# Early tiles' choices inside the retention, a reordered list, and weight loads that wait for the first gather

## The chip, the cores and the metric

One core of one Trainium2 chip runs the whole program. The metric is device time in microseconds (us), the median of several runs. TensorE (PE in the rows) does matrix products, with the loading of its weights as PEld; VectorE (DVE), ScalarE (ACT) and GpSimd (POOL) do elementwise work; SyncE (SP) issues most DMAs. Each engine works through its own instructions in order and waits for the others by semaphores. 16 DMA engines move all data between HBM and the on-chip memory.

## What is computed

Three stages follow each other. The middle one is a mixture of experts with a capacity, assigned greedily over all logits:

```python
scores = (q @ k.T) / sqrt(64) * decay          # retention, 8 heads, causal decay
x = (scores @ v)                               # 2304 tokens x 512
logits = x @ w_gate                            # 8 experts
for idx in argsort(-logits.flatten()):         # strongest pair first
    tok, e = idx // 8, idx % 8
    if assigned[tok] >= 0 or counts[e] >= 288: continue
    assigned[tok] = e; counts[e] += 1
for e in range(8):
    out[mask_e] = maximum(x[mask_e] @ w1[e], 0) @ w2[e]     # 512 -> 1024 -> 512
h = out @ w_in                                 # 512 -> 2048
result = (h * tanh(log1p(exp(h)))) @ w_out     # 2048 -> 512
```

## The kernel before

**Retention.** 18 tiles of 128 tokens run one after the other. For tile t the loop (lines 280 to 289) issues loads, the scores of tile t+1, the outputs of tile t, the running state, and `turn(t - 1)`: that transposes the tile, adds its logits to `L` (a VectorE reduction, line 254) and stores its rows of x to `x_scratch`. The order of PE, DVE and POOL here is the order of the program text.

**Routing.** The greedy assignment is done expert by expert in the order in which they fill up. `choices` (L350 to L355) finds each token's best open expert with five small DVE instructions, `reached` (L361) compares each best logit with 63 thresholds into the table `G`, and TensorE counts with `pF` (L305, L445) how many tokens of each expert lie above each. Six such steps (`route`, DVE table `G` L427, PE `pF`, DVE `sat`, PE `pD`) narrow down the threshold at which the next expert is full. `weights_of` then reads that expert's number (`eid`) and loads its weights, and `tokens` makes the list of its 288 tokens: comparisons, the table `ohb` in two halves (L587), the PE product `pI` (L595), the list `chosen` (L599). Three indirect DMAs on POOL (L607) gather the rows of x (`xg`), PE transposes them (`mmx`), and ACT and DVE split them into a rounded part and a rest (`xh`, `xl`).

**Experts.** Each expert needs eight weight units of 512 KB (`st`, line 543): four of w1, four of w2. ACT rounds a unit (`whi`, L557); POOL or DVE forms the rest (`wlo`, L560). Every product takes three TensorE passes (high by high, low by high, high by low): `mma` is the first layer, `mmb` the second, 96 matmuls each. A unit of w1 serves two of the first layer's eight blocks. Five staging buffers (`STAGES`) hold loaded units. Beside this, `narrow` turns the last stage's weights from 64-bit words into f32 (`std`, `words`, `dw`, `dt`), a piece at a time.

**The planner.** After the retention the order on every engine is made by a list scheduler at build time (`run_tasks`). A task yields (engine, assumed duration in ns, what it waits for, priority); the smallest start time goes first, and a task steps back for one of smaller priority number that would be ready before it ends. Assumed times only set the order. Among them are `LATE` (8,000 ns, added to the arrival of most loads) and `GATHER` (10,000 ns from the gather's issue to its rows). Before expert 0's first product PE runs dummy products (`warm`).

Of the kernel before, what the change touches and what calls it, by code (L numbers as in the profile page):

```python
# [17 lines left out]
P = 128  # L18
# [8 lines left out]
HP = H // 2  # L27
WARM = 11
STRADDLE = (4, 13)

# [15 lines left out]
LATE = 8000  # L46
GATHER = 10000
SCATTER = 3200
FIRST = 163
# [83 lines left out]
class Kernel:  # L133
# [3 lines left out]
    def attention(self):  # L137
# [10 lines left out]
        with ExitStack() as st:  # L148
# [129 lines left out]
            scale(1, nc.gpsimd)  # L278
            scale(2, nc.gpsimd)
            for t in range(NT - 1):  # L280
                load(t + 3)
                scale(t + 3, nc.gpsimd)
                scores(t + 1)
                carried(t, Sb[seen[0] % 2])
                outputs(t)
                state(t)
                turn(t - 1)
                if t == 6:
                    self.routing_consts()
            t = NT - 1  # L290
            carried(t, Sb[seen[0] % 2])
            outputs(t)
            turn(t - 1)
            self.psum = lambda name, shape: ps.tile(shape, F32, name=name, tag="pS" if name == "pF" else "pA", bufs=1 if name == "pF" else 2)
            G = self.rw.tile([P, NT, 64], BF16, name="G")
            self.chosen = self.rw.tile([GB, E, 3], I32, name="chosen", bufs=1)
            pF = self.psum("pF", [64, E])
            early, late = slice(0, t - 1), slice(t - 1, NT)
            choice = self.choices(early)
            self.reached(choice, G, early)  # L300
            turn(t)
# [41 lines left out]
    def choices(self, ts=slice(0, NT), into=None):  # L343

        pool, v, L = self.rw, self.nc.vector, self.L
        both = [P, ts.stop - ts.start, E]
        if into is None:
            into = [self.at("raw"), pool.tile([P, NT], F32, name="top"), pool.tile([P, NT, E], BF16, name="oh")]
        raw, top, oh = (x[:, ts] for x in into)
        v.tensor_reduce(raw, L[:, ts], AX.X, ALU.max)  # L350
        cand = self.at("cand").rearrange("p (t e) -> p t e", e=E)[:, ts]
        v.tensor_tensor(cand, L[:, ts], raw[:, :, None].to_broadcast(both), op=ALU.is_equal)
        v.tensor_tensor(cand, cand, self.rc[:, None, RC["prio"]].to_broadcast(both), op=ALU.mult)
        v.tensor_reduce(top, cand, AX.X, ALU.max)
        v.tensor_tensor(oh, cand, top[:, :, None].to_broadcast(both), op=ALU.is_equal)  # L355
        return into

# [11 lines left out]
    def route(self):  # L369
# [8 lines left out]
        for i in range(E):  # L378
# [102 lines left out]
            if i:  # L481
                self.widen(i, ohe)
                self.spawn(self.weights_of(junk, at, i))
                choice = yield from self.choose(i, at)
            at = yield DVE, 1600, [marked, at], 0
            pose = rw.tile([P, NT], F32, name="pose")
            v.scalar_tensor_tensor(pose, scan[:, 1], pP[:, 1:2], eq, op0=ALU.add, op1=ALU.mult)
            v.scalar_tensor_tensor(pos, scan[:, 0], pP[:, 0:1], gt, op0=ALU.add, op1=ALU.mult)
            fin = self.at("fin")
            v.scalar_tensor_tensor(fin, pose, CAP + 0.5, eq, op0=ALU.is_lt, op1=ALU.mult)  # L490
            if i == 0:
                self.spawn(self.weights_of(junk, at, i))
            v.tensor_tensor(self.dead, self.dead, gt, op=ALU.add)
            v.tensor_tensor(self.dead, self.dead, fin, op=ALU.add)
            v.tensor_tensor(pose, pose, fin, op=ALU.mult)
            v.tensor_tensor(pos, pos, pose, op=ALU.add)
            self.spawn(self.tokens(i, pos, at))
            if i == 0:
# [11 lines left out]
    def choose(self, i, at):  # L510
        if i == E - 2:
            return None
        yield DVE, 1750, [at], 0
        return self.choices()

    def weights_of(self, junk, at, i):
# [11 lines left out]
        for u in range(8):  # L528
            if u < 4:
                src = a["w1"][bass.ds(e, 1), :, u * 256:(u + 1) * 256]  # L530
            else:
                src = a["w2"][bass.ds(e, 1), (u - 4) * 256:(u - 3) * 256, :]
            yield from self.unit(n0 + u, src.rearrange("o (k p) c -> p (o k) c", p=P),
                                 DVE if n0 == 0 and u < 2 else None, units, 3,
                                 *([lambda: self.fetched] if n0 == 0 and u == FIRST_UNITS else []))

    def unit(self, n, src, eng, into, prio, *after):
# [4 lines left out]
        st = self.stage.tile([P, 1024], F32, name="st")  # L542
        self.nc.sync.dma_start(st.rearrange("p (k c) -> p k c", k=src.shape[1]), src)
        self.loaded[n] = at
        self.spawn(self.split_unit(n, st, self.arrival(524288, at, LATE if 1 < n < E * 8 else DMA_WAIT), eng, into, prio))

    def split_unit(self, n, st, at, eng, into, prio):
# [10 lines left out]
        self.rounded[n] = hi  # L558
        lo = yield ({POOL: 2480, DVE: 1240} if eng is None else eng), 1240, [hi], prio
        (self.nc.vector if lo.engine == DVE else self.nc.gpsimd).tensor_tensor(dst[1], st, dst[0].bitcast(F32), op=ALU.subtract)  # L560
# [3 lines left out]
    def tokens(self, i, pos, at):  # L564
# [24 lines left out]
        for ts, made in zip(halves, ready):  # L589
            at = yield PE, 740, [made, side, *([] if pI is not None else [self.bank])], pr  # L590
            if pI is None:
# [14 lines left out]
        for j in range(3):  # L606
            nc.gpsimd.indirect_dma_start(out=xg[:, j], out_offset=None, in_=a["x"],  # L607
                                         in_offset=bass.IndirectOffsetOnAxis(ap=idx[:, j:j + 1], axis=0))
        at = Event(at.t + GATHER)
        if i > 1:  # L610
# [499 lines left out]
```

## Time and profile before

| | us |
|---|---|
| median of 3 runs (lowest, highest) | 813.99 (812.19, 814.79) |
| profiled execution | 809.8 |
| its span, first to last instruction | 808.0 |
| PE busy | 766.4 (95% of the span) |
| DVE busy | 668.5 (83%) |
| POOL busy | 464.4 (57%) |
| ACT busy | 413.2 (51%) |
| mean granted TensorE clock | 0.982 of full |

The span is one profiled execution; its own time is a little above its span. Busy time of an engine counts its instructions, not its waits. The retention ends at about 84 us, expert 0's products start at 126.03 us, and the last stage begins to dominate after about 390 us.

### The profile page before, as it was taken

Reading aid. Unit: us, or ns where it says so; the run is one execution under the profiler, and the core shown is the slowest. Engines: PE = TensorE matmul, PEld = TensorE weight load, DVE = VectorE, ACT = ScalarE, POOL = GpSimd, SP = SyncE. Lnnn points to the kernel's source line nnn. Section 1 sums busy time; section 2 is a strip of 40 time slices with the busy share of each in tenths; the row PEclk is TensorE's granted clock in tenths of the full one; section 3 lists DMA queues with packets and bytes.
Section 4 is the critical chain, followed back from the end, with each engine's and each line's share of the span. In section 5 each row is a group of like instructions: output and inputs, shape, how many; then the busy total and the mean of one; then the engine's idle time right before and its main releaser. Section 6 shows DMA issues by size and latency. Waiting matters only on the chain.

```text
span 808.0 us, 16171 instructions
## 1 busy us (share of the span) xinstructions
PE 766.4 (95%) x6184; PEld 688.3 (85%) x6184; DVE 668.5 (83%) x1089; ACT 413.2 (51%) x781; POOL 464.4 (57%) x402
## 2 busy tenths in 40 slices
PE   7999479999999999799899899999999999999996
PEld 5898338898999989799898788898899988999985
DVE  2444687897988888696698999989998998998993
ACT  1233115556555565575664455555556556555552
POOL 3653035779797796340166776657466566655644
PEclk9999789999999999899999999999999999999999
DMA  9993165888888887986700010001001001000001
GB/s 342 408 354 129 41 208 184 265 264 283 252 290 251 299 265 229 331 270 231 247 1 21 20 40 21 12 21 47 2 20 40 19 21 40 20 1 13 27 1 39
DMA packets 61117, 112.52 MB, mean 139 GB/s; under 512 B 4848, under 2 KB 33008, under 8 KB 61040
## 3 DMA queue, kind: packets, MB, share of 16 engines
q1 hardware_dynamic: 44816, 74.00, 26.8%
q10 hardware_dynamic: 13248, 28.06, 10.4%
q0 software_dynamic: 2976, 9.44, 3.6%
q8 instruction: 48, 0.79, 0.4%
q14 instruction: 29, 0.24, 0.1%
HBM read 88.93 MB, written 22.54 MB: 138 GB/s over the span
## 4 chain that ended last, share of the span: by engine, by line
PE 59%; DVE 8%; DMA 2%; POOL 2%; issue 2%; ACT 1%; SPq 0%; POOLq 0%; ACTq 0%; DVEq 0%
PE mmc L987 23%; PE po L1048 21%; PE mmb L771 7%; PE mma L771 7%; DVE q L1017 2%; DMA st<-w 1%; PE pF L445 1%; DVE hl L797 1%; DVE ohb L587 1%; DVE wlo L560 1%; DVE G L427 1%; DMA st<-w_out 1%; POOL n L1019 1%; POOL gl L1029 1%; DVE n L1012 1%
## 5 line engine op out<-in xcount | busy, mean ns | idle before, releaser
L1017 DVE RECIPROCAL q<-q 128x384 f32<-128x384 f32 x96 | 244.3, 2545 | 11.3 <-ACT q L1015 9.7
L1019 POOL TENSOR_TENSOR n<-n,q 128x384 f32<-128x384 f32 x96 | 99.3, 1034 | 140.3 <-DVE q L1017 137.7
L1029 POOL TENSOR_TENSOR gl<-n,gh 128x384 fp32r<-128x384 f32 x96 | 105.4, 1098 | 50.5 <-ACT gh L1027 50.1
L987 PE MATMUL mmc<-yl,whi 128*128 128x384 f32 x384 | 130.2, 339 | 4.3 <-POOL yl L947 2.5
L987 PE MATMUL mmc<-yh,whi 128*128 128x384 f32 x384 | 130.0, 339 | 0.6 <-ACT yh L944 0.5
L987 PE MATMUL mmc<-yh,wlo 128*128 128x384 f32 x384 | 129.7, 338 | 0.0
L560 POOL TENSOR_TENSOR wlo<-st,whi 128x1024 fp32r<-128x1024 f32 x49 | 116.9, 2400 | 13.1 <-ACT whi L557 12.4
L1048 PE MATMUL po<-whi,gh 128*128 128x512 f32 x288 | 114.0, 396 | 0.0
L1048 PE MATMUL po<-whi,gl 128*128 128x512 f32 x288 | 113.9, 395 | 0.0
L1048 PE MATMUL po<-wlo,gh 128*128 128x512 f32 x288 | 113.3, 393 | 0.0
L1005 ACT ACTIVATE s<-mmc 128x384 f32<-128x384 f32 x96 | 47.1, 491 | 122.2 <-PE mmc L987 119.2
L1012 DVE SCALAR_TENSOR_TENSOR n<-s 128x384 f32<-128x384 f32 x96 | 103.3, 1076 | 2.1 <-ACT s L1005 1.2
L557 ACT CAST whi<-st 128x1024 fp32r<-128x1024 f32 x80 | 82.0, 1043 | 40.5 <-DMA st<-w 31.6
L771 PE MATMUL mma<-xh,whi 128*128 128x288 f32 x256 | 77.5, 303 | 3.0 <-DVE xl L620 3.0
L987 PEld LDWEIGHTS mmc<-yl,whi 128*128 128x128 f32 x384 | 72.1, 188 | 9.5 <-POOL yl L947 3.4
L771 PE MATMUL mmb<-hl,whi 128*128 128x288 f32 x256 | 77.9, 304 | 0.0
L771 PE MATMUL mmb<-hh,whi 128*128 128x288 f32 x256 | 77.4, 302 | 0.0
L771 PE MATMUL mmb<-hh,wlo 128*128 128x288 f32 x256 | 77.3, 302 | 0.0
L987 PEld LDWEIGHTS mmc<-yh,whi 128*128 128x128 f32 x384 | 72.1, 188 | 5.5 <-ACT yh L944 1.5
L771 PE MATMUL mma<-xh,wlo 128*128 128x288 f32 x256 | 76.7, 300 | 0.0
L771 PE MATMUL mma<-xl,whi 128*128 128x288 f32 x256 | 76.6, 299 | 0.0
L987 PEld LDWEIGHTS mmc<-yh,wlo 128*128 128x128 f32 x384 | 72.2, 188 | 0.0
(146 smaller groups left out, 1541.2 us busy)
## 6 DMA issues: line engine op xcount, KB each, us to landing
st<-w SPq DMA_DIRECT2D x64, 512.0 KB, 5.7
qk<-qk SPq DMA_DIRECT2D x18, 512.0 KB, 7.9
kv<-kv SPq DMA_DIRECT2D x18, 512.0 KB, 8.1
std<-w_out ACTq DMA_DIRECT2D x15, 512.0 KB, 5.1
std<-w_in ACTq DMA_DIRECT2D x14, 512.0 KB, 5.3
x_scratch<-xs SPq DMA_DIRECT2D x18, 256.0 KB, 4.1
y_scratch<-y ACTq DMA_DIRECT2D x32, 144.0 KB, 3.9
yt<-y_scratch SPq DMA_DIRECT2D x22, 192.0 KB, 2.4
```

Of the source, the lines that this page charges most:

```text
L427: v.tensor_tensor(G[:, :, :m], key[:, :, None].to_broadcast([P, NT, m]), T[:, None, :].to_broadcast([P, NT, m]), op=ALU.is_ge)
L445: nc.tensor.matmul(pF[:m, :], G[:, t, :m], oh[:, t, :], start=(t == 0), stop=(t == NT - 1))
L557: self.nc.scalar.copy(dst[0], st)
L560: (self.nc.vector if lo.engine == DVE else self.nc.gpsimd).tensor_tensor(dst[1], st, dst[0].bitcast(F32), op=ALU.subtract)
L771: self.nc.tensor.matmul(bank[1][:, :CAP], al if h == 2 else ah, bl if h == 1 else bh, start=(first and j == h == 0), stop=(last and j == n ...
L987: self.nc.tensor.matmul(bank[1][:, :TILE], (wl if h == 2 else wh)[:, c, cs], x[c][h == 1], start=(c == h == 0), stop=(c == HP - 1 and h == 2))
L1005: nc.scalar.activation(s, p, AF.Sigmoid)
L1012: v.scalar_tensor_tensor(u, s, 2.0, s, op0=ALU.subtract, op1=ALU.mult)
L1017: v.reciprocal(q, q)
L1019: nc.gpsimd.tensor_tensor(u, u, q, op=ALU.mult)
L1029: nc.gpsimd.tensor_tensor(gl, u, gh.bitcast(F32), op=ALU.subtract)
L1048: nc.tensor.matmul(po[j], (gl if h == 2 else gh)[:, js], (wl if h == 1 else wh)[:, f % 2], start=(f == h == 0), stop=(f == DFF // P - 1 an ...
```

## The change

Five edits are made together.

1. The choices and the first threshold table of tiles 0 to 8, 9 to 12 and 13 to 15 are made inside the retention loop, right after `turn` of the last of them, rather than for tiles 0 to 15 in one go after `turn(16)` and ahead of `turn(17)`. The last two tiles are done after `turn(17)` as before.
2. In `route`, the two updates of `dead` come after the positions that the list needs, and in a request of their own; `choose` of expert 0 is split into two requests; the planner assumes 480 ns for `pI` rather than 740.
3. The `wlo` of expert 0's units 0 and 1 goes from DVE to POOL, and is planned after the gather.
4. The load of unit 2 of expert 0 (`FIRST_UNITS` is 2) gets a semaphore wait on the last of the first gather's three DMAs. SP issues in order, so all later loads follow it.
5. The planner assumes 3,000 ns (`GATHERED`) for the first gather's landing rather than 10,000, and plans unit 2 after that.

```diff
+EARLY = (9, 13, 16)
+GATHERED = 3000
...
+            G, choice = self.rw.tile([P, NT, 64], BF16, name="G"), None
             for t in range(NT - 1):
...
+                if t in EARLY:
+                    ts = slice(max([0] + [e for e in EARLY if e < t]), t)
+                    choice = self.choices(ts, choice)
+                    self.reached(choice, G, ts)
...
-            early, late = slice(0, t - 1), slice(t - 1, NT)
-            choice = self.choices(early)
-            self.reached(choice, G, early)
+            late = slice(EARLY[-1], NT)
             turn(t)
             self.choices(late, choice)
...
-            at = yield DVE, 1600, [marked, at], 0
+            at = yield DVE, 1250, [marked, at], 0
...
             v.scalar_tensor_tensor(fin, pose, CAP + 0.5, eq, op0=ALU.is_lt, op1=ALU.mult)
+            v.tensor_tensor(pose, pose, fin, op=ALU.mult)
+            v.tensor_tensor(pos, pos, pose, op=ALU.add)
             if i == 0:
                 self.spawn(self.weights_of(junk, at, i))
+            self.spawn(self.tokens(i, pos, at))
+            at = yield DVE, 350, [at], 0
             v.tensor_tensor(self.dead, self.dead, gt, op=ALU.add)
             v.tensor_tensor(self.dead, self.dead, fin, op=ALU.add)
-            v.tensor_tensor(pose, pose, fin, op=ALU.mult)
-            v.tensor_tensor(pos, pos, pose, op=ALU.add)
-            self.spawn(self.tokens(i, pos, at))
...
-        yield DVE, 1750, [at], 0
-        return self.choices()
+        if i:
+            yield DVE, 1750, [at], 0
+            return self.choices()
+        at = yield DVE, 650, [at], 0
+        parts = self.choice_parts()
+        into = next(parts)
+        yield DVE, 1000, [at], 0
+        next(parts, None)
+        return into
...
-                                 DVE if n0 == 0 and u < 2 else None, units, 3,
-                                 *([lambda: self.fetched] if n0 == 0 and u == FIRST_UNITS else []))
+                                 POOL if n0 == 0 and u < FIRST_UNITS else None, units, 3,
+                                 *([lambda: self.fetched and Event(self.fetched.t + GATHERED)] if n0 == 0 and u == FIRST_UNITS else []))
...
+        if n == FIRST_UNITS:
+            self.tc.add_manual_dep(d.ins, self.gathering.name, mybir.DependencyInfo(mybir.DependencyClass.Sync, mybir.DependencyReason.DATA),
+                                   reason="the first expert's rows go ahead of its later weights")
...
-        lo = yield ({POOL: 2480, DVE: 1240} if eng is None else eng), 1240, [hi], prio
+        lo = yield ({POOL: 2480, DVE: 1240} if eng is None else eng), 2480 if eng == POOL and n < E else 1240, [hi, *([lambda: self.fetched] if n < FIRST_UNITS else [])], prio
...
-            at = yield PE, 740, [made, side, *([] if pI is not None else [self.bank])], pr
+            at = yield PE, 480, [made, side, *([] if pI is not None else [self.bank])], pr
...
-        at = Event(at.t + GATHER)
+        at = Event(at.t + (GATHER if i else GATHERED))
```

`choice_parts` is `choices` as a generator that pauses after the `is_equal` of L352; `choices` runs it to its end.

## Rows read from the trace of the kernel before

**Rows 1.** Stages: from:to length, PE PEld DVE ACT POOL busy, clock, DMA share, GB/s.
```profile
80.00:126.00 46.00, 28.37 (x341) 17.56 (x340) 32.88 (x119) 7.31 (x15) 6.27 (x4) 0.81 0.45 148
126.00:330.00 204.00, 201.41 (x1948) 187.38 (x1946) 174.60 (x550) 117.41 (x205) 161.21 (x93) 1.00 0.79 256
330.00:340.00 10.00, 4.74 (x28) 3.95 (x28) 4.28 (x7) 5.18 (x11) 1.27 (x1) 0.77 1.06 387
340.00:808.00 468.00, 456.95 (x2397) 415.19 (x2396) 422.55 (x343) 261.03 (x486) 258.79 (x255) 1.00 0.16 53
```

**Rows 2.** Timeline at the retention's end: start, duration, engine, line, operation [idle before].
```profile
82.15 2.12 PE L252 MATMUL pX<-both,xT 128*128 128x136 f32 x16
83.47 0.28 DVE L350 TENSOR_REDUCE sc<-L 128x16 f32<-128x128 f32 x1
...
84.98 1.20 DVE L361 TENSOR_TENSOR G<-sc,rc 128x1008 bf16<-128x1008 f32 x1
86.10 0.17 DVE L254 TENSOR_REDUCE L<-pX 128x8 f32<-128x16 f32 x1
```

**Rows 3.** Timeline inside the retention, at tile 15.
```profile
69.41 1.29 DVE L204 TENSOR_TENSOR am<-pA,mask 128x512 f32<-128x512 f32 x2 [0.85 <-PE pA L201]
```

**Rows 4.** Timeline from the first decision to the list of expert 0.
```profile
104.91 0.17 DVE L493 TENSOR_TENSOR dead<-dead,sc 128x18 f32<-128x18 f32 x1
...
109.22 0.57 PE L595 MATMUL pI<-R,ohb 128*96 128x6 bf16 x9 [0.16 <-DVE ohb L587]
...
110.81 0.15 DVE L599 TENSOR_REDUCE chosen<-pI 96x3 int32<-96x6 f32 x1
```

**Rows 5.** Timeline from the first gather to expert 0's first product.
```profile
111.24 1.10 POOL L607 DMA_INDIRECT xg<-x_scratch,chosen  x1 [39.98 <-DMA st<-w]
...
114.71 1.07 POOL L607 DMA_INDIRECT xg<-x_scratch,chosen  x1 [0.30 <-issue]
...
126.03 0.38 PE L771 MATMUL mma<-xh,whi 128*128 128x288 f32 x1
```

**Rows 6.** DMA of 114 to 118 us: queue shares, and issue to landing.
```profile
q0 software_dynamic: 84, 0.28, 23.1%
...
xg<-x_scratch,chosen POOLq DMA_INDIRECT x2, 8.6
```

**Rows 7.** DMA of 310 to 345 us: the last two experts' gathers.
```profile
xg<-x_scratch,chosen POOLq DMA_INDIRECT x6, 3.8
```

**Rows 8.** The gathers (tile xg) over the span: issue durations, and landing.
```profile
L607 POOL DMA_INDIRECT xg<-x_scratch,chosen x24: 917/921/1961, 111.2 to 323.3; - x24
...
DMA to landing us min/median/max: 3.1/5.0/8.8
```

**Rows 9.** The staged weights (tile st), 100 to 150 us: landing.
```profile
DMA to landing us min/median/max: 3.5/6.7/10.2
```

**Rows 10.** The page's groups: cost of rounding a unit and of its rest.
```profile
L560 POOL TENSOR_TENSOR wlo<-st,whi 128x1024 fp32r<-128x1024 f32 x49 | 116.9, 2400 | 13.1 <-ACT whi L557 12.4
...
L557 ACT CAST whi<-st 128x1024 fp32r<-128x1024 f32 x80 | 82.0, 1043 | 40.5 <-DMA st<-w 31.6
```

**Rows 11.** Timeline of ACT in expert 0's first layer: blocks three and four.
```profile
132.43 0.41 ACT L794 ACTIVATE hh<-mma 128x288 fp32r<-128x288 f32 x1 [1.48 <-PE mma L771]
134.18 0.41 ACT L794 ACTIVATE hh<-mma 128x288 fp32r<-128x288 f32 x1 [1.34 <-PE mma L771]
```

**Rows 12.** Timeline of PE where expert 1 begins.
```profile
159.76 0.66 PE L628 MATMUL mmx<-cst,xg 96*128 96x96 f32 x6
...
160.83 0.30 PE L771 MATMUL mma<-xh,whi 128*128 128x288 f32 x1
```

**Rows 13.** The chain that ended last, in the steady part: start, duration, what.
```profile
218.03 0.73 PE pF L445 x18
```

**Rows 14.** Timeline of POOL: the first multiplication of `narrow`.
```profile
148.38 1.29 POOL L754 TENSOR_TENSOR dw<-dw,dt 128x512 f32<-128x512 f32 x1
```

**Rows 15.** Timeline of PE: expert 0's second layer, its 37th matmul.
```profile
147.55 0.30 PE L771 MATMUL mmb<-hh,whi 128*128 128x288 f32 x1
```

More of the change, by code (lines that the diff above doesn't have):

```diff
@@ L294, in attention @@
             self.psum = lambda name, shape: ps.tile(shape, F32, name=name, tag="pS" if name == "pF" else "pA", bufs=1 if name == "pF" else 2)
-            G = self.rw.tile([P, NT, 64], BF16, name="G")
             self.chosen = self.rw.tile([GB, E, 3], I32, name="chosen", bufs=1)
             pF = self.psum("pF", [64, E])
-            early, late = slice(0, t - 1), slice(t - 1, NT)
-            choice = self.choices(early)
-            self.reached(choice, G, early)
+            late = slice(EARLY[-1], NT)
             turn(t)
@@ L343, in choices, with choice_parts @@
     def choices(self, ts=slice(0, NT), into=None):
+        parts = self.choice_parts(ts, into)
+        into = next(parts)
+        next(parts, None)
+        return into
+    def choice_parts(self, ts=slice(0, NT), into=None):
         pool, v, L = self.rw, self.nc.vector, self.L
@@ L352, in choices @@
         v.tensor_tensor(cand, L[:, ts], raw[:, :, None].to_broadcast(both), op=ALU.is_equal)
+        yield into
         v.tensor_tensor(cand, cand, self.rc[:, None, RC["prio"]].to_broadcast(both), op=ALU.mult)
@@ L355, in choices @@
         v.tensor_tensor(oh, cand, top[:, :, None].to_broadcast(both), op=ALU.is_equal)
-        return into
     def reached(self, choice, G, ts):
@@ L512, in choose @@
             return None
-        yield DVE, 1750, [at], 0
-        return self.choices()
+        if i:
[3 more added lines that the diff above has]
+        parts = self.choice_parts()
+        into = next(parts)
+        yield DVE, 1000, [at], 0
+        next(parts, None)
+        return into
     def weights_of(self, junk, at, i):
@@ L542, in unit @@
         st = self.stage.tile([P, 1024], F32, name="st")
-        self.nc.sync.dma_start(st.rearrange("p (k c) -> p k c", k=src.shape[1]), src)
+        d = self.nc.sync.dma_start(st.rearrange("p (k c) -> p k c", k=src.shape[1]), src)
+        if n == FIRST_UNITS:
+            self.tc.add_manual_dep(d.ins, self.gathering.name, mybir.DependencyInfo(mybir.DependencyClass.Sync, mybir.DependencyReason.DATA),
+                                   reason="the first expert's rows go ahead of its later weights")
         self.loaded[n] = at
@@ L606, in tokens @@
         for j in range(3):
-            nc.gpsimd.indirect_dma_start(out=xg[:, j], out_offset=None, in_=a["x"],
+            d = nc.gpsimd.indirect_dma_start(out=xg[:, j], out_offset=None, in_=a["x"],
                                          in_offset=bass.IndirectOffsetOnAxis(ap=idx[:, j:j + 1], axis=0))
-        at = Event(at.t + GATHER)
+        self.gathering = d.ins
+        at = Event(at.t + (GATHER if i else GATHERED))
         if i > 1:
```

## The prediction, made before the result

> **What bounds the kernel now.** I read the table of stages first. In the last stage, from 340 us, PE is busy for 457 of 468 us; while the experts are worked through beside the routing, from 126 to 330 us, it is busy for 201.4 of 204. The change touches neither's work. Between the retention's end and the first product PE is busy for only 28.4 of 46 us, dummy products included, and from 330 to 340 us for 4.7 of 10 [rows 1]. So a start of expert 0's products that comes earlier by some us is worth as much at the end, unless a wait behind it takes it back. The timelines of those 46 us then show one chain: the retention's last choices, the threshold search, the list, the gather, the first product. The reader is to see in them which piece of work stood in front of which [rows 2, 4, 5]. The DMA views say why the rows of the gather were late [rows 6 to 9].
>
> **What it takes off that chain.** (1) PE ends the last `turn` at 82.15 + 2.12 = 84.27, but DVE adds that tile's logits only at 86.10, since the choices and the table of sixteen tiles run from 83.47 to 84.98 + 1.20 = 86.18 in front of it [rows 2]. With those made before, the reduction can start at about 84.35: 1.75 us. The moved work, 2.7 us in one go, comes as three pieces of nine, four and three tiles. I cost it at nothing, because DVE idles 0.85 us ahead of each tile's `am` [rows 3] and the nine-tile piece, by its share of 2.7 some 1.5 us and with its fixed costs perhaps 2, delays one `am` by about 1 us, which is needed a tile later. If that cover is gone the three cost at most 3 x (2 - 0.85), 3.5 us; bounds 0 and 3.5, and I take 0.
>
> (2) The two updates of `dead`, 0.17 us each, stood in front of the positions [rows 4]: 0.3 us. The list's end, `chosen`, started at 110.81 although PE had finished its counts at 109.22 + 0.57 = 109.79 [rows 4]: DVE was in the five instructions of the next choice, one request of 1,750 ns for the planner. Split in two, with 480 ns for the product, the list is ready for the planner before the first half would end, so it goes first: 1.0 us. The other experts' lists also gain 0.3 each, beside a busy PE; I count nothing for them.
>
> (3) The three gathers started 114.71 - 111.24 = 3.47 us apart from first to last, 0.30 of it idle ahead of the third [rows 5]; one takes 0.92 as a rule, though up to 1.96 [rows 8]. DVE's two `wlo` ran beside these three; they leave. At the usual pace the third starts after 2 x (0.92 + 0.30) = 2.4; I take 2.6, a gain of 0.85, bounds 0 and 1.0.
>
> (4) Landing. The first gathers took a median of 8.6 us, in a window whose other traffic was weights [rows 6]. The last two experts' gathers took 3.8 [rows 7]; the quickest of all 3.1, the median 5.0 [rows 8]. With only two weight units ahead of them, I take 3.8: a gain of 4.8, bounds 3.6 and 5.5. The share of the gather's queue in that window is 23.1% [rows 6]. The Trainium skill, page "DMA: Bandwidth & Descriptors", section "Queues, rings and completion order", says that each DMA engine takes turns between the queues that have work, a packet at a time. By that rule a gather with a queue of its own needn't be protected from another queue's weights, and the whole 4.8 would be in doubt; the measured share and the two landing times speak for protection, and the trace does not separate them from other causes.
>
> Together 1.75 + 0.3 + 1.0 + 0.85 + 4.8 = 8.7 us: the first product would start at 117.3 rather than 126.03 [rows 5].
>
> **What it adds.** (a) Unit 2 waits. The gather starts at 111.24 - 3.05 = 108.2, its third DMA at 110.8, and lands at 114.6; only then does SP issue unit 2 and, behind it, units 3 to 7 and the first three loads of `narrow`. Landing takes 3.5 us at best and 6.7 at the median [rows 9], rounding 1.04, the rest on POOL 2.40 [rows 10]: ready at 121.6 to 124.8. The fifth block of the first layer needs it. The fourth block's activation came at 134.18, 8.15 us after the first product [rows 5, 11], so the need is at about 117.3 + 8.15 = 125.4. That alone would be no wait. But the planner still adds `LATE`, 8,000 ns, to the unit's arrival, and so puts its rounding on ACT behind the third block's activation. That one came 6.4 us after the start [rows 11], now 123.7 to 124.1; rounding ends at 125.2, the rest at 127.6: PE waits 2.2 us. Behind the fourth activation it would be 3.9. Bounds 0 and 3.9, I take 2.2.
>
> (b) Before, PE ran five of the six `pF` steps of expert 1's search while it had nothing else to do; with an earlier start some three of them fall beside products, at 0.73 us each [rows 13]: 2.2 us if all of it is new PE time, 0 if they fall into the waits (a) and (c), which are longer together. I take 1.0.
>
> (c) PE now reaches expert 1 earlier, but expert 1's list does not come earlier by as much: its search gains the 1.75, 0.3 and 1.0, and DVE loses two splits, yet it now shares DVE with expert 0's work. Before, the transposes of expert 1 stood inside expert 0's last products, 1.07 us ahead of the first `mma` [rows 12]. If they come behind them, PE waits for their splitting; from landed rows to the first product expert 0 needed 126.03 - (114.71 + 8.6) = 2.7 [rows 5, 6]. Bounds 0 and 2.7, I take 1.5.
>
> (d) POOL gets 2 x 2.40 = 4.8 us of splits [rows 10]. Units 0 and 1 are split from about 112 to 117, before the first product needs the second of them; the cover is the gather's flight.
>
> So 8.7 - 2.2 - 1.0 - 1.5 = 4.0 us less: 805.8 against the profiled execution's 809.8. That execution lay below the median of the runs, 813.99; I take the same difference from the median: 810.0.
>
> **The rivals.** *The lead arrives whole.* Unit 2 is rounded in time and the search keeps up, so (a) and (c) vanish: 8.7 - 1.0 = 7.7, 806.3; with the bounds of the gains, 0.15 + 0.7 more, and part of the 2.6 us in which PE idled from 126 to 330 [rows 1], 803.5. For it: the unit's data are there 0.6 us or more ahead of need. Against it: ACT is in order and the planner's 8,000 ns stand.
>
> *The wait at expert 6 swallows it.* From 330 to 340 us PE idles 5.3 us while the DMA engines are fully busy [rows 1]. If the transfers there keep their place on the clock, PE merely arrives earlier and waits longer; perhaps 1 us stays: 813.0. Against it: the DMA share is 0.79 on average before, so there is room for an earlier transfer.
>
> *The gather is no faster.* If the gather's queue already got its turns beside the weights and the 8.6 had another cause, the 4.8 goes; the waits shrink with the lead, (a), (b) and (c) to about 2 in all: 8.7 - 4.8 - 2 = 1.9 less at best, some 1 to 2, about 813. The 23.1% of a queue that had three transfers waiting [rows 6] makes that unlikely. It is the rule of the Trainium skill's page "DMA: Bandwidth & Descriptors" ("Queues, rings and completion order") taken at its word.
>
> *Slower: POOL becomes the bound of expert 0.* Six units are split on POOL, 6 x 2.40 = 14.4 us [rows 10]. Where the first starts at 127, behind the fourth activation, and three multiplications of `narrow` at 1.29 [rows 14] come between, the last unit is done at 127 + 14.4 + 3.9 = 145.3, and the gather of expert 1 stands behind it on POOL. The second layer needs that unit for its 37th matmul, which came 147.55 - 126.03 = 21.5 us after the first product [rows 5, 15], now 138.8: 6.5 us of waiting. If expert 1's rows come late by the gather's own issue too, (c) is at its bound of 2.7. 8.7 - 6.5 - 2.2 - 2.7 = 2.7 slower: 816.7. It decides once the waits of (a), (b), (c) together pass 8.7. Against it: a split takes 2.40, and PE used a unit of w1 in two blocks, 8.15 / 2 = 4.1 us [rows 11], so a late start is caught up.
>
> **How the numbers follow.** Forecast 0.49, own range 808.0 to 812.0; lead whole 0.16; swallowed 0.14; gather no faster 0.06; slower 0.15. About 0.3%, 2.4 us, is what a measurement of this kernel can tell from no change. Of the forecast's 0.49 some 0.05 lie within it: faster 0.44 + 0.16 = 0.60, same 0.05 + 0.14 + 0.06 = 0.25, slower 0.15. The range reaches from the lead's far end, 803.5, to 816.0, about the middle of the slower case, and leaves out some 0.15.
>
> **What would show it.** The last tile's logits at about 84.4; `chosen` at about 107.8; gathers landing in 3 to 5 us; first `mma` near 117.3; an idle of about 2 us on PE ahead of the fifth block, ended by a `wlo` of POOL; the first `mma` of expert 1 at about 155 (before: 160.83); the idle of 330 to 340 us at its former length, moved forward. It is wrong if the first `mma` comes after 120, if PE waits for units 3 to 7 as well, or if expert 6 begins when it began before.

## The result, and the profile after

The changed kernel took 825.15 us (median of 4 runs, 824.65 to 829.36) against 813.45 before in the same session: a ratio of 1.0146, 95% interval 1.0119 to 1.0172. The profiled execution took 824.65, its span 822.9. The forecast of 810.0, and its range to 816.0, were wrong.

The windows of the changed kernel, with the columns of [rows 1]:

```profile
80.00:126.00 46.00, 31.06 (x355) 22.40 (x353) 30.93 (x119) 10.14 (x21) 9.47 (x6) 0.81 0.41 144
126.00:330.00 204.00, 192.62 (x1827) 178.75 (x1827) 159.07 (x528) 102.08 (x173) 148.55 (x84) 0.95 0.70 228
330.00:340.00 10.00, 10.00 (x87) 10.00 (x85) 9.20 (x10) 7.71 (x21) 6.09 (x5) 1.00 0.87 269
340.00:900.00 560.00, 465.86 (x2428) 423.97 (x2426) 436.56 (x360) 271.41 (x503) 267.50 (x261) 0.98 0.17 57
```

The second row is the one to read. While the experts run, PE was busy for 192.6 us rather than 201.4, and its granted clock was 0.95 rather than 1.00 [rows 1]. At two levels, 1.2 and 2.4 GHz, 0.95 over 204 us means, as an estimate, 204 x 0.05 x 2 = 20.4 us at the lower one, 10.2 us of products lost. With 8.8 us more of idling that is 19 us, in a stretch that the forecast took as untouched.

The start, where the forecast looked, did what it said. The timeline of the changed kernel at its start: the last tile's logits, the list, the gather's three issues, the transposes, the first product:

```profile
83.98 0.17 DVE L256 TENSOR_REDUCE L<-pX 128x8 f32<-128x16 f32 x1 [0.75 <-PE pX L254]
...
107.43 0.16 DVE L621 TENSOR_REDUCE chosen<-pI 96x3 int32<-96x6 f32 x1 [0.38 <-PE pI L617]
107.87 1.10 POOL L629 DMA_INDIRECT xg<-x_scratch,chosen  x1 [36.93 <-DVE sc L361]
...
110.51 0.92 POOL L629 DMA_INDIRECT xg<-x_scratch,chosen  x1 [0.30 <-issue]
...
113.68 0.91 PE L651 MATMUL mmx<-cst,xg 96*128 96x96 f32 x9
...
116.62 0.38 PE L794 MATMUL mma<-xh,whi 128*128 128x288 f32 x1 [0.26 <-ACT xh L641]
```

The first product came at 116.62, 9.4 us earlier than before [rows 5]. Expert 1's first `mma` came at 161.37, 0.5 later than before [rows 12]: the lead was gone within expert 0. The last stage's first `mmc` came at 394.86; before, 385.37.

### The profile page after: what moved, and what is told of

The parts are those of the page before. It is cut to its first block, busy times and chain, and to the rows that moved or that the text cites. A ratio compares the mean times of both kernels' runs of the same rounds, so it can differ in the third digit from the quotient of the medians.

```text
span 822.9 us, 16132 instructions
## 1 busy us (share of the span) xinstructions
PE 772.2 (94%) x6170; PEld 698.0 (85%) x6170; DVE 672.9 (82%) x1099; ACT 413.6 (50%) x781; POOL 468.5 (57%) x404
## 4 chain that ended last, share of the span: by engine, by line
PE 68%; DVE 17%; issue 5%; DMA 4%; ACT 2%; POOL 2%; ACTq 1%; SPq 0%; POOLq 0%; DVEq 0%
PE mmc L1010 17%; PE po L1071 16%; PE mma L794 11%; PE mmb L794 10%; DVE q L1040 6%; DVE n L1035 3%; PE pF L456 3%; PE pX L254 2%; PE pT L240 2%; PE pA L203 2%; DVE G L438 1%; DVE n L1045 1%; DMA qk<-qk 1%; DMA st<-w 1%; POOL n L1042 1%
## 5 line engine op out<-in xcount | busy, mean ns | idle before, releaser
L582 POOL TENSOR_TENSOR wlo<-st,whi 128x1024 fp32r<-128x1024 f32 x51 | 120.9, 2389 | 17.8 <-ACT whi L579 17.8
L1071 PE MATMUL po<-wlo,gh 128*128 128x512 f32 x288 | 113.9, 395 | 0.0
L794 PE MATMUL mma<-xh,whi 128*128 128x288 f32 x256 | 80.7, 315 | 2.5 <-DVE xl L643 2.2
L794 PE MATMUL mma<-xl,whi 128*128 128x288 f32 x256 | 79.7, 311 | 0.0
L794 PE MATMUL mma<-xh,wlo 128*128 128x288 f32 x256 | 79.1, 309 | 0.0
L777 POOL TENSOR_TENSOR dw<-dw,dt 128x512 f32<-128x512 f32 x32 | 43.9, 1373 | 61.1 <-ACT dt L767 50.6
```

The lines of the kernel that those rows point to most:

```text
L777: nc.gpsimd.tensor_tensor(out, out, t, op=ALU.mult)
L794: self.nc.tensor.matmul(bank[1][:, :CAP], al if h == 2 else ah, bl if h == 1 else bh, start=(first and j == h == 0), stop=(last and j == n ...
L1071: nc.tensor.matmul(po[j], (gl if h == 2 else gh)[:, js], (wl if h == 1 else wh)[:, f % 2], start=(f == h == 0), stop=(f == DFF // P - 1 an ...
```

## The experiments

Eighteen kernels ran, in five sets. Each ratio is against runs of the kernel before on the same chip; intervals are 95%. Sets may be on different chips, so small differences are read within a set. A search step is one round of `G`, `pF`, `sat` and `pD`; a pocket, in the expectations, is a short idle time of PE.

**First set: which edit.** Edit 1 alone (`x1`), edits 1 and 2 (`x2`), all but the planner's 3,000 ns (`x4`), all but the semaphore (`x3`):

```diff
x4
-        at = Event(at.t + (GATHER if i else GATHERED))
+        at = Event(at.t + GATHER)
x3
-        if n == FIRST_UNITS:
-            self.tc.add_manual_dep(d.ins, self.gathering.name, mybir.DependencyInfo(mybir.DependencyClass.Sync, mybir.DependencyReason.DATA),
-                                   reason="the first expert's rows go ahead of its later weights")
```

> The kernel before with the early choices alone. The order that the planner writes for the experts is the one of before, instruction by instruction. Theory A (the new order of the later experts' search steps leaves PE short pockets, each followed by a stretch at the lower clock): the order is unchanged, so the 1.75 us of the start arrive whole, 811.7. Theory B (any earlier start of expert 0 only makes PE run into work that has not come earlier, pockets and half clock included): the gain is swallowed, 813 to 816. Theory C (the late weights and their splits on POOL): not touched here, 811.7.

> The kernel before with the early choices and the new list (its order, the choice of expert 0 in two requests, 480 ns for the list's products), without the edits of the gather, the late weights and POOL. Its first product can start some 3 us earlier. From the second expert's list on the planner's order on PE is that of the changed kernel. Theory A: the later experts lose what they lost in the changed kernel, 213.2 - 205.1 = 8.1 us from expert 1 to expert 7 and 448.4 - 442.0 = 6.3 behind it, so 813.45 - 3 + 14.4 = 825, no less than 819. Theories B and C, by which the loss comes from expert 0's weights and gather: 813.45 - 3 = 810.4, or 813 if the lead is swallowed.

> The changed kernel, with the planner's time for the landing of expert 0's gather at 10,000 ns again; the wait of the later weights stays. Two more of expert 1's search steps then stand ahead of the first product, which starts at some 122 rather than 116.6, but expert 0 has no search step in its first blocks, and its pockets of 1.3, 1.7 and 1.5 us go. Theory A: expert 1 begins at 158 to 161 as against 161.4, the later experts as in the changed kernel: 822 to 825. Theory B or C with expert 0 as the place of the loss: expert 1 at 157 and then the pace of before, 813.45 - 3.8 = 809.6.

> The changed kernel without the wait of the first expert's later weights for the gather on the chip; the planner's order is the same, so only the start of unit 2's transfer differs, and the gather shares the DMA engines with weights again. Theory A: the gather lands up to 4.8 us later, the first product starts at 117 to 121, unit 2 is there earlier, and the rest is as in the changed kernel: 823 to 826. Theory C (the late units and what follows from them cost the lead): the pocket of 1.26 us ahead of the fifth block and its half clock go, and with them most of the loss, 811 to 816.

`x1` 810.17 us, 0.9956 (0.9932 to 0.9981). `x2` 824.73, 1.0116 (1.0083 to 1.0148). `x4` 826.29, 1.0124 (1.0061 to 1.0188). `x3` 832.93, 1.0194 (1.0125 to 1.0263). The early choices pay; adding the list edit turns a gain into nearly the whole loss, with no edit of the gather at all. Theory C fell: without the wait it is no faster. The wait does protect the gather: from the third issue to the first product 6.1 us with it (110.51 to 116.62 above), 8.7 without. Timeline of `x3`:

```profile
112.46 0.92 POOL L626 DMA_INDIRECT xg<-x_scratch,chosen  x1 [0.30 <-issue]
...
121.20 0.61 PE L791 MATMUL mma<-xh,whi 128*128 128x288 f32 x1
```

What the wait is worth to the rows themselves stands in point (4) below.

**Second set: the list edit for expert 0 alone.** `x5` is the changed kernel, `x6` is `x2`, `x7` is `x4`, each with the old request and the old order of its instructions for experts 1 to 7:

```diff
+            if i:
+                at = yield DVE, 1600, [marked, at], 0
...
+            else:
+                at = yield DVE, 1250, [marked, at], 0
...
-            at = yield PE, 480, [made, side, *([] if pI is not None else [self.bank])], pr
+            at = yield PE, 740 if i else 480, [made, side, *([] if pI is not None else [self.bank])], pr
```

`x8` is the changed kernel with the gathers of experts 1 to 7 issued later:

```diff
+        if i:
+            nc.gpsimd.memset(xg, 0.0)
+            nc.gpsimd.memset(xg[:, 0, :384], 0.0)
```

> The changed kernel, with the list's new order and its 480 ns for expert 0 alone; the other experts' lists are asked for as before the change. Theory A (the later experts' new order costs the 14.4 us behind expert 1): from expert 2 on the order on PE is nearly that of before, the pockets of 0.9 to 1.7 us ahead of pD go, and 825.15 - 14.4 = 810.8; expert 0 still loses its 9.4 us of lead, since its search steps stand among its first products. Rival (the pockets come from PE being early, whatever the order): 822 to 826.

> The early choices and the new list for expert 0 alone, nothing of the gather, the weights and POOL. Theory A: the order behind expert 1 is nearly that of before, and the further 0.3 and 1.0 us of the start arrive beside the early choices' gain: 810.17 - 1.3 = 808.9. Rival (every gain of the start beyond the early choices is given back at expert 1, which waits for its own search): 810 to 812. If the split list itself is the loss: 822 to 825.

> As the run before this one, and with the wait of the later weights for the gather and the splits of units 0 and 1 on POOL, but 10,000 ns for the gather in the planner. The planner's two extra search steps ahead of the first product decide its start, not the gather: near 124, as in the run with 10,000 ns above. Theory A: 809 to 811, the wait of the weights neither pays nor costs as long as the planner does not use it. Theory C (late weights cost by themselves): 813 or more, and PE waits for units 2 to 7.

> The changed kernel, its order on PE and DVE unchanged, with two fills of the gather's target by POOL ahead of the gathers of experts 1 to 7 (some 1.9 us by the rate of the fill of 512 elements in 0.53 us). They put the gather as late behind the first search step as it was before the change: there the first gather was issued 0.1 us ahead of the end of pF, in the changed kernel 2.0 us ahead. Theory D (the step's result reaches DVE late because the gather's rows are moving just then): the pockets of 1.7, 0.9, 1.7 and 1.7 us ahead of pD of step 0 go, with them their half clock, 6.0 + 4 x 1.7 = 12.8 us, so 812 to 815. Theory A in its plain form (the order on PE alone makes the pockets): they stay, 825 to 827.

`x5` 819.19, 1.0062 (1.0033 to 1.0091). `x6` 814.48, 0.9996 (0.9967 to 1.0024). `x7` 814.53, 0.9998 (0.9970 to 1.0026). `x8` 825.86, 1.0130 (1.0071 to 1.0190). So the later experts' list is worth 0.8 to 1.3% with or without the gather edits, but `x5` came back only half as far as expected. `x6` missed its 808.9: the early choices' gain is not seen in it, though its interval and that of `x1`, from another chip, overlap. In `x8` the idle times ahead of the first `pD` shrank to 0.75 to 1.53 us, but in three of the four places 1.0 us came back ahead of the next `pF`, and the time stayed. So theory D missed its price, but it was hardly tested: POOL made the fills before the list was ready and then waited. Timeline of `x8`:

```profile
145.89 0.41 POOL L630 MEMSET xg<- 96x384 f32 x1
147.56 0.16 DVE L621 TENSOR_REDUCE chosen<-pI 96x3 int32<-96x6 f32 x1 [0.85 <-PE pI L617]
148.48 0.93 POOL L632 DMA_INDIRECT xg<-x_scratch,chosen  x1 [2.17 <-DVE chosen L621]
```

The gather's first issue came 0.92 us behind `chosen`, in the changed kernel 0.43 (143.04 to 143.47): it moved by 0.5 us and not by 1.9.

**Third set: the list's order, its 480 ns, and two waits.** `x9` is `x2` with 740 ns, `x10` is `x6` with 480 for all, `x11` is `x5` with 5,000 ns for expert 1's gather, `x12` is the changed kernel without `LATE` on units 2 to 7:

```diff
x11
-        at = Event(at.t + (GATHER if i else GATHERED))
+        at = Event(at.t + (GATHERED if i == 0 else 5000 if i == 1 else GATHER))
x12
-   LATE if 1 < n < E * 8 else DMA_WAIT
+   LATE if 7 < n < E * 8 else DMA_WAIT
```

> The early choices and the list's new order for all experts, but 740 ns in the planner for the list's products as before; nothing of the gather, the weights and POOL. On PE each later expert's transposes stand ahead of one more search step, as in the changed kernel. If it is the list's order (the updates of dead behind the list, as a request of their own) that costs the 9.8 us between the run with the new list for all and the one with it for expert 0: 822 to 825. If it is the 480 ns: 813 to 816. Half and half: 819.

> The other half of the pair: the new order of the list for expert 0 alone, and 480 ns for the list's products of all experts. On PE the later experts' transposes stand behind the last but one search step, as before the change. If the list's order costs the 9.8 us: 813 to 816. If it is the 480 ns: 822 to 825.

> The changed kernel with the list's new order for expert 0 alone, and 5,000 rather than 10,000 ns in the planner for the landing of expert 1's gather. Expert 1 began at 159 to 167 us in all ten traces, wherever expert 0 began. Theory E (expert 1 begins there because the planner puts its transposes behind search steps of expert 2 on which PE waits, with the rows long landed): the transposes come ahead of such a step, the pocket of 1.58 us and its half clock go, expert 1 begins 3 us earlier, 819.2 - 3 = 816. Rival (the search on DVE sets the pace, and PE waits for the step behind the transposes instead): 819 to 821.

> The changed kernel, with the planner's 8,000 ns off the arrival of expert 0's units 2 to 7 (2,000 in its place), so that ACT rounds unit 2 ahead of the third block's activation. Step (a) of the prediction: the pocket of 1.26 us ahead of the fifth block goes, with the half clock behind it, 825.15 - 1.26 - 1.7 = 822. Rival (expert 1 does not begin earlier, so that the time is only waited out elsewhere in expert 0): 825.

`x9` 828.50, 1.0170 (1.0125 to 1.0214). `x10` 805.24, 0.9885 (0.9862 to 0.9908). `x11` 813.15, 0.9989 (0.9973 to 1.0004). `x12` 827.94, 1.0178 (1.0119 to 1.0237). The list's order, with the request of its own that it brought, is the cost, and 480 ns, far from costing, pays. In `x11` expert 1 began at 157.92 rather than 161.71. In `x12` the idle ahead of the fifth block went and the first layer took 17.0 us rather than 19.5, but expert 1 began at 161.91: the time was waited out later.

**Fourth set: put together.** `x14` is the changed kernel with the old list for experts 1 to 7 (480 stays), `x15` is `x7` with 480 for all, `x16` is `x14` with 5,000 ns for expert 1's gather, `x17` is edit 1 and 480 ns alone.

> The changed kernel with the list's new order for expert 0 alone (480 ns for all, gather and weights as in the changed kernel): the one step that the pair before this points to is undone, all else stays. The planner's order does not become regular here: the third later expert still has its transposes ahead of a search step. Theory A (the list's order costs most of it): 825.15 - 10 = 815. Rival (the loss comes from the gather's 3,000 ns just as much): 818 to 822.

> The kernel of 805.24 us (early choices, new list for expert 0 alone, 480 ns for all), and with the wait of the later weights for the gather and the two splits on POOL, but 10,000 ns for the gather in the planner. Its order behind expert 1 is the same. If the wait and POOL neither pay nor cost: 805. If the weights that come later cost: 808 or more.

> All that the change holds for expert 0, its early start too, with the list's order of before for the others, and 5,000 ns for the landing of expert 1's gather in the planner, as expert 0's lead could otherwise not reach expert 1. From expert 2 on the order is the regular one of the kernel of 805.24 us. Theory E: expert 1 begins at 157.9 as in the run with 5,000 ns above, then 220.3 us to the last stage and 421.6 behind it as in that kernel: span 799.8, some 802.5. Rival (nothing of expert 0's lead passes expert 1): 805 to 808.

> The early choices and 480 ns for the list's products, nothing else of the change; the list's order is that of before for all experts. Its order behind expert 1 is the regular one of the kernel of 805.24 us. If the regular order alone is what made that kernel faster: 804 to 806. If the new list of expert 0 is needed for it: 809 to 811.

`x14` 810.79, 0.9974 (0.9947 to 1.0002). `x15` 799.33, 0.9819 (0.9785 to 0.9853). `x16` 800.59, 0.9856 (0.9816 to 0.9896). `x17` 800.96, 0.9872 (0.9824 to 0.9921). The last three beat both kernels; among themselves they can't be told apart. `x17` shows how little is needed. From 160 to 325 us its PE never idles, at full clock, and DVE gets more done than in the changed kernel (second row):

```profile
160.00:325.00 165.00, 165.00 (x1599) 154.94 (x1599) 144.34 (x453) 94.93 (x170) 132.09 (x78) 1.00 0.83 270
```

```profile
160.00:325.00 165.00, 157.48 (x1497) 145.88 (x1496) 130.81 (x434) 82.87 (x144) 121.14 (x68) 0.96 0.70 231
```

**Fifth set: which part of the list's order.** `x18`: the new order of the seven instructions, but one request of 1,600 ns. `x19`: the request of its own stays, but the next search's keys get the list's priority.

```diff
x19
-                at = yield DVE, 180, [at], 0
+                at = yield DVE, 180, [at], -1
```

> The changed kernel with its new order of instructions in the list (the updates of dead last), but the seven in one request of 1,600 ns as before, and the list's own task started behind it. The planner's order on PE is that of the run with 810.79 us (0.9974 of before). Theory A, now narrowed: not the instructions' order costs, but that the updates are a request of their own, behind which the next search's first table falls in the planner's time; 808 to 813. Rival (the dead updates behind the positions delay the next search by themselves): 818 or more.

> The changed kernel, updates of dead as a request of their own included, with one number changed: the request for the next search's keys has the list's priority, so that DVE makes the first table of the next search ahead of the end of the list again, as before the change. Theory A, narrowed (what costs is the table behind the list's end; the step's products then come some 2 us after the gather's issue rather than beside it): the pockets ahead of the first pD go, 807 to 815. Rival (the place of this table is a sign of the new order and not its cost): 820 to 826.

`x18` 818.80, 1.0051 (1.0018 to 1.0084); `x19` 818.51, 1.0062 (1.0037 to 1.0087). Neither theory's numbers were met: each run gives back 0.8 to 1.0 of the changed kernel's 1.46%, about half of what the old list gives (`x14`). `x18` also starts the list's own task behind the updates, and `x19`'s one number moves other work on PE as well, so which part of the edit costs how much is not settled by these two.

## Why the prediction was wrong

**The step that failed** is in part (2): "The other experts' lists also gain 0.3 each, beside a busy PE; I count nothing for them." The ratios, by list (rows) and by what was done with the gather (columns):

| list's order, planner's time for `pI` | gather edits left out | wait, POOL, 10,000 ns | wait, POOL, 3,000 ns |
|---|---|---|---|
| new for all, 480 | 1.0116 | 1.0124 | 1.0146 (the change) |
| new for expert 0, 740 | 0.9996 | 0.9998 | 1.0062 |
| new for expert 0, 480 | 0.9885 | 0.9819 | 0.9974 |

From the first row to the third each column falls by 1.7 to 3.1%, 14 to 25 us (the rows come from different sets; the intervals do not touch). Edit 2 as it was made, from `x1` to `x2` in one set, cost 0.9956 to 1.0116, some 13 us, where the forecast had a gain of 1.3 at the start and nothing behind it. With 740 for all and the new order for all (`x9`) it is 1.0170, so 740 is no way out.

Where the time went, in the profiled executions: expert 0 began 9.4 us earlier and took 9.95 longer; from the first product of expert 1 to that of expert 7 it took 213.2 us rather than 205.1, 8.1 longer; expert 7 took 0.9 and the last stage 5.4 longer. Together that is 14.9 us, the difference of the spans. The forecast had terms, of 4.7 together, for the 9.95 alone.

How it costs is seen on DVE and PE. The updates of `dead` were made a request of their own. The planner then placed the first table `G` of the next search behind the end of the list. Timeline of the changed kernel, expert 3's list:

```profile
216.58 0.16 DVE L621 TENSOR_REDUCE chosen<-pI 96x3 int32<-96x6 f32 x1 [0.46 <-PE pI L617]
216.66 1.33 DVE L438 TENSOR_TENSOR G<-sc,rc 128x1134 bf16<-128x1134 f32 x1
217.01 0.94 POOL L629 DMA_INDIRECT xg<-x_scratch,chosen  x1 [3.87 <-DVE chosen L621]
...
218.30 0.75 PE L456 MATMUL pF<-oh,G 128*63 128x8 bf16 x18
...
221.23 0.16 DVE L377 TENSOR_SCALAR sat<-pF 63x8 bf16<-63x8 f32 x1 [1.73 <-PE mmb L794]
221.44 0.16 PE L461 MATMUL pD<-sat,digit 63*128 63x8 bf16 x1 [1.68 <-DVE sat L377]
```

The same place in the kernel of 805.24 us, where `G` comes first as it did before the change:

```profile
212.91 1.32 DVE L437 TENSOR_TENSOR G<-sc,rc 128x1134 bf16<-128x1134 f32 x1
214.16 0.15 DVE L632 TENSOR_REDUCE chosen<-pI 96x3 int32<-96x6 f32 x1
214.48 0.75 PE L455 MATMUL pF<-oh,G 128*63 128x8 bf16 x18
214.58 0.94 POOL L640 DMA_INDIRECT xg<-x_scratch,chosen  x1 [3.93 <-DVE chosen L632]
...
215.95 0.16 DVE L376 TENSOR_SCALAR sat<-pF 63x8 bf16<-63x8 f32 x1
216.16 0.16 PE L460 MATMUL pD<-sat,digit 63*128 63x8 bf16 x1 [0.20 <-DVE sat L376]
```

From the list's end to the first `pD` took 4.9 us above and 2.0 below. The first search step of four experts left PE idle, 1.69, 0.93, 1.68 and 1.66 us ahead of `pD`. The place of the table makes no idle by itself: in `x14` it also stood behind the list of expert 3, the step's result came on time, and `pD` followed without an idle (last section). The idles come where a step's result is late, and in these kernels the late steps ended while POOL issued a gather or just behind it; that section has the count over all traces. `x19` puts `G` in front again and gains 0.8%, which fits, but its order on PE differs in other places too. Two things follow from the idles.

First, the clock. Timeline of PE in the changed kernel behind one of these idle times, then windows of the whole stretch:

```profile
147.92 0.16 PE L461 MATMUL pD<-sat,digit 63*128 63x8 bf16 x1 [1.69 <-DVE sat L377]
...
148.65 0.29 PE L794 MATMUL mmb<-hh,wlo 128*128 128x288 f32 x1
...
149.13 0.44 PE L794 MATMUL mmb<-hh,wlo 128*128 128x288 f32 x1
```

```profile
130.00:148.00 18.00, 16.31 (x153) 15.41 (x152) 12.96 (x48) 6.51 (x11) 12.19 (x8) 0.95 0.58 187
148.00:160.00 12.00, 10.21 (x101) 9.21 (x101) 8.81 (x27) 5.93 (x10) 8.65 (x6) 0.82 0.75 228
160.00:170.00 10.00, 10.00 (x84) 9.10 (x83) 7.02 (x26) 3.92 (x10) 6.70 (x4) 0.70 0.49 170
```

A product takes 0.29 us right behind the idle and 0.44 a microsecond later. From 160 to 170 us PE was busy all the time and did 84 instructions; at a clock of 0.70 that is 3 us lost where the busy share shows nothing. The forecast priced idles at their own length. Not every idle is followed by this: the one at 221.44 above is not (last section).

Second, `narrow`. DVE and ACT got through less between 126 and 330 us, so the last piece of the last stage's weights was made at 398.0; before it was 356.1, in the kernel of 805.24 us 353.4. Two rows of the tile `dw`, the changed kernel and that one, the last figures first and last start:

```profile
L777 POOL TENSOR_TENSOR dw<-dw,dt x32: 1268/1292/2163, 146.9 to 398.0; 128x512 f32<-128x512 f32 x32
```

```profile
L787 POOL TENSOR_TENSOR dw<-dw,dt x32: 1268/1294/2296, 148.0 to 353.4; 128x512 f32<-128x512 f32 x32
```

It now stands in the last stage's start, and PE idles there. Timeline of the changed kernel:

```profile
394.86 0.44 PE L1010 MATMUL mmc<-yh,whi 128*128 128x384 f32 x1 [0.96 <-ACT yh L967]
399.81 0.69 PE L1010 MATMUL mmc<-yl,whi 128*128 128x384 f32 x1 [4.51 <-DVE yl L970]
```

From the first `mmc` to the end took 428.0 us, before 422.6; in `x2`, `x3`, `x4`, `x8` and `x9`, which have the new list for all too, 427.1 to 428.2, and in `x12` 425.5, all with the last piece at 398 us or later. In `x18` and `x19`, with the last piece at 373.3 and 366.5, it took 422.9 and 422.7. The late piece is not the only cause: `x1` and `x5` took 425.9 and 425.7 with theirs at 356.8 and 364.8.

**Why the 9.4 us never reached expert 1.** The premise in the first part was that an earlier start "is worth as much at the end, unless a wait behind it takes it back". Starts from the timelines of the profiled executions:

| kernel | first product | expert 1 | last stage | span |
|---|---|---|---|---|
| before | 126.03 | 160.83 | 385.37 | 808.0 |
| the change | 116.62 | 161.37 | 394.86 | 822.9 |
| `x14` | 117.75 | 160.51 | 383.29 | 805.9 |
| `x15` | 123.27 | 159.28 | 378.00 | 800.8 |
| `x16` | 117.70 | 156.05 | 376.27 | 798.9 |
| `x17` | 124.53 | 158.87 | 376.91 | 797.3 |

With expert 1's gather planned at 10,000 ns, expert 1 starts at 158.9 to 166.6 in every kernel, whether expert 0 starts at 116 or 126. An early expert 0 merely takes 42 to 45 us instead of 34 to 38: its products meet the search of expert 1, and that did not come sooner: `chosen` of expert 1 started at 142.4 to 148.2 us in all twenty traces. So 3,000 ns in the planner cost 0.6% in the second set and 1.5% in the fourth (`x7` to `x5`, `x15` to `x14`). With 5,000 ns for the next gather too, expert 1 starts at 156 to 158, and the ratio falls by 0.7% (`x5` to `x11`) and 1.2% (`x14` to `x16`): part of the lead arrives.

**Point by point.** (1) Logits at 83.98 (forecast 84.4), and `x1`, which has this edit alone, began its products 1.9 us earlier (124.11) and gained 0.44% (0.19 to 0.68): right. The upper bound of 3.5 is reckoned wrongly, since it takes off the cover of 0.85 that it supposes gone; without it, it would be 6. (2) `chosen` at 107.43 (107.8): right for expert 0. (3) third issue 2.64 behind the first (2.6): right, but `x2`, whose two `wlo` stay on DVE and come behind the third issue, has 2.64 as well, so the new list's order was enough for it. (4) first product at 116.62 (117.3): right, and the landing too. The changed kernel's trace does not record it; the first gather's issue to landing in `x14`, which has the wait, and in `x17`, which has not:

```profile
DMA to landing us min/median/max: 3.1/3.1/3.3
```

```profile
DMA to landing us min/median/max: 6.8/7.5/8.3
```

By the packets of the gather's queue, its last row came 2.6 to 2.8 us behind the start of the third issue in each of the twelve traces with the wait (the changed kernel 2.65), and 4.7 to 9.5 in each of the eight without (before 7.27, `x3` 4.65). So the gain of 4.8 was about right (7.27 - 2.65 = 4.6), and the rival by which the gather is no faster is out. Between `x3` and the changed kernel, which differ in the wait alone, it is 2.0. The early start needs the planner's 3,000 ns as well: in `x4` the last row's packet ended at 113.9, and the first product only at 124.57, behind search steps that the planner had put in front. The Trainium skill, page "DMA: Bandwidth & Descriptors", section "Queues, rings and completion order", has the engines take turns between queues, a packet at a time. The prediction took from it that by this rule the whole 4.8 would be in doubt; these runs show 2 to 7 us for the wait.

(a) The idle ahead of the fifth block was 1.26 us (2.2), but a table of the search ended it, not a `wlo`. Timeline of the changed kernel:

```profile
123.03 1.99 ACT L579 CAST whi<-st 128x1024 fp32r<-128x1024 f32 x2
124.14 4.72 POOL L582 TENSOR_TENSOR wlo<-st,whi 128x1024 fp32r<-128x1024 f32 x2 [8.03 <-ACT whi L579]
126.39 0.61 PE L456 MATMUL pF<-oh,G 128*31 128x8 bf16 x18 [1.26 <-DVE G L438]
```

Unit 2 was rounded behind the third activation, as forecast; the planner put two search steps in front of the block; without its 8,000 ns (`x12`) this idle went. (b) The search steps came beside the products. (a), (b) and (c) together were forecast at 4.7 us; expert 0 grew by 44.75 - 34.80 = 9.95, with two more idles (1.69 and 1.54 us) and the lower clock: they were forecast at half their size. Of (c), expert 1 at 155 was wrong by 6.4 us. (d) Right: `x15` splits on POOL and loses nothing. Expert 6 began 7.6 us later than before (342.08, before 334.44), which was named as a sign of a wrong forecast in a milder form. The slower rival had the sign right and the place wrong. POOL was not the bound of expert 0: the three idles over 1 us in it were ended by `G`, `sat` and `known`, all of the search on DVE, and none by a `wlo`.

## What to carry to other kernels

Where a list scheduler writes the order, a planned time or a new request is an edit of everything behind it: compare the order that it writes for the later rounds before pricing only the first. A lead at the start counts only if the next hand-over can move too; look at when the second round starts, not the first. Price an idle of TensorE with the clock that follows it.

## What was not expected of the hardware

Idles of 1.3 to 1.9 us on a busy PE were mostly followed by a stretch at the lower clock (windows above). In the changed kernel, from 120 to 330 us, there were six of 1.26 to 1.88 us: four were followed by one, and so was an idle of 0.93; those that ended at 221.44 (1.68) and 256.36 (1.66) were not. Before, idles of 0.5 to 0.65 us were not, while in `x6` a stretch began at 250.8 us behind an idle of only 0.26.

A search step's result sometimes reached DVE late. In the changed kernel `pF` ended at 218.30 + 0.75 = 219.05, DVE was free at 219.50, and `sat` started at 221.23. Behind expert 0's list `x14` and `x18` have the same order on PE, and on DVE but for two small updates; the same step in `x18` and then in `x14`:

```profile
218.83 1.33 DVE L438 TENSOR_TENSOR G<-sc,rc 128x1134 bf16<-128x1134 f32 x1
...
220.46 0.75 PE L456 MATMUL pF<-oh,G 128*63 128x8 bf16 x18
...
223.44 0.16 DVE L377 TENSOR_SCALAR sat<-pF 63x8 bf16<-63x8 f32 x1 [1.79 <-remote]
223.66 0.16 PE L461 MATMUL pD<-sat,digit 63*128 63x8 bf16 x1 [1.73 <-DVE sat L377]
```

```profile
212.40 1.33 DVE L438 TENSOR_TENSOR G<-sc,rc 128x1134 bf16<-128x1134 f32 x1
...
214.04 0.75 PE L456 MATMUL pF<-oh,G 128*63 128x8 bf16 x18
...
215.14 0.15 DVE L377 TENSOR_SCALAR sat<-pF 63x8 bf16<-63x8 f32 x1
...
215.45 0.18 PE L461 MATMUL pD<-sat,digit 63*128 63x8 bf16 x1
```

That is 2.2 us behind the end of `pF` against 0.35, though the gather's issues lie alike. By the traces' semaphore events, behind 126 us, the changed kernel has four search steps whose result came 1.4 to 2.2 us late. The other six kernels with the new list for all (`x2`, `x3`, `x4`, `x8`, `x9`, `x12`) have three to five that came more than 1 us late, `x18` one, `x19` two, and the remaining eleven, the kernel before included, none but one of 1.0 us in `x6`. Every one of them ended 0.1 to 1.2 us behind the start of one of a gather's issues on POOL. Steps that ended 1.9 us or more behind the last issue came at most 0.11 us late, though the rows still moved; so it is the time of issuing that they share, and not the moving rows. `x14`'s step above lies beside the issues as `x18`'s does and was on time, so that is not enough either.

In the changed kernel the signal of the products behind `pF` on PE came late together with that of `pF` (221.26 and 221.20). The ends of matmuls in these rows are modelled, so PE itself may have finished later than they show. What holds the result back stays open; `x8` does not settle it, since its gather was still being issued when `pF` ended. Open too is how much of the fourth set's gain is owed to its absence: `x14` and `x18`, in sets on different chips, differ by 0.8%, which the order of two small updates does not explain.
